# A state-space scan and a routed expert layer: rows turned by transposes, logits in column tiles, one-hots of places on ScalarE, first halves without zero blocks

## The chip, the cores and the metric

The kernel runs on one core of a Trainium2 chip. The metric is the device time of one execution in microseconds; the time of a kernel is the median of several executions. A profile is taken of one further execution, and every time inside the kernel below comes from it, counted from the start of its span.

## The reference

Two layers follow each other. The first is a chunked state-space scan over 4 batches, 8 heads, 768 steps, head width 32, state width 16. Per chunk:

```
cum = cumsum(log a);  L = exp(cum_i - cum_j), lower triangle
y   = ((C B^T) * L) x  +  (C state) * exp(cum)
state = exp(sum log a) * state + sum_j B_j x_j exp(cum_last - cum_j)
```

Its output, seen as 3072 rows (batch, step) of 256 columns (head, width), goes to a router with 8 experts:

```
logits = normalised rows @ normalised expert_emb^T / tau
e      = argmax(logits);  gate = softmax(logits)[e]
out    = gate * (relu(row @ w1[e]) @ w2[e])        # 256 -> 1024 -> 256
```

All is float32.

## The kernel before, in words

**Scan.** The 768 steps are cut in 6 blocks of 128 (`c`), each over all 4 batches and 8 heads. The loop is in `mamba` (L745 to L849), and its order is written out by hand[...]. A block has these steps. `load` brings C, B (two layouts) and x by SyncE's queue; x comes whole as `x`, and the second half of its columns for the first 64 steps once more as `xa`, on partitions 64 to 127 (L68). `scale_c` (VectorE, L254) multiplies C by the decays that `spread_decays` put in PSUM. `inner` (TensorE, L362) makes the products of C and B for two batches at a time in `pg`; `mask_inner` (VectorE, L372) takes them out as `g`, 128x1536. A block has two of these, g(c,0) and g(c,1); the second `inner` of a block waits for `scale_c` of the next. `scale_x` and `scale_first_half` (GpSimd, L276, L289) scale x by inverse decays, into `xs` and `xb`. `from_states`, `outputs` and `first_outputs` (L383, L400, L413) sum y, transposed, in `py`: columns on partitions, in the order (half row r, half v, width), 128 per half z. `first_outputs` is for the first 64 steps of a block: `xb` holds for each head pair a block with zeros in it, so that one product of 128x64 weights gives two heads. Two `xb` buffers are cleared once each, by `clear_first_half` on VectorE. `keep_outputs` (ScalarE, L424) takes y out as `yT`. The states are carried through `sums`, `add_sums` (`V`, VectorE), `decay_states` (`T` on VectorE, `U` on GpSimd, L324).

**Rows and routing.** `finish` (L427) of a block stands in the next block: 8 products of `yT` with `turn` (L432), a matrix that both turns and reorders the columns and holds the normalised expert vectors beside them, so that 128 columns and 8 logits come out together. `keep_rows` (ScalarE, L441, L443) and `send_rows` write rows of 264 columns to memory. `pick` (VectorE) finds each row's expert, `count_picks` (GpSimd) and `rank_rows` (TensorE) its rank; `keep_ranks` (ScalarE, L578) takes that out. `places` (VectorE, L581 to L617) turns the rank into a place: `ge`, `pl`, `eq`, and last `hot`, a one-hot of 104 places for 4 batches (L614). It stands at the end of block c for the rows of block c-2. `locate` (TensorE, L624) multiplies `hot` with `eq` into a table of row numbers, 104 places by 32 (expert, tile), in bank `pz[0]`; ScalarE keeps it (`keep_located`), GpSimd adds (`add_located`). In the last block `early_places` (L913) reads row numbers from the first three blocks' table for the first experts' rows, before g(5,0) in VectorE's queue.

**Scan's end and experts.** `scan_end` (L853) mixes the last blocks' routing with the first expert job: `first.up(f)` (8 products with w1, L1045, relu on ScalarE, L1049), then `down(0)`, `down(1)` (L1063). Their PSUM banks `eb` rotate over 4 buffers: turn_x, up 0 to 7, turn_x of the second job, down(0), down(1), so that down(0) takes the bank that up(5) had. `places` of block 3 stands in the loop's last round, of blocks 4 and 5 in `scan_end`; `locate` of blocks 3 and 4 follows up(3), of block 5 down(0), and `end_places` (L643) makes the final table `idx`. The experts (`moe`, L1315 on) then run one after another, each with rows gathered by GpSimd's indirect transfers, weights through `load_weights` (w1 in two pieces of 64 partitions, L94) and rows scattered to the output.

Of the kernel before, what the change touches and what calls it, by code (L numbers as in the profile page):

```python
# [51 lines left out]
def load(k, c):  # L52
    nc = k.nc
    t = k.ld[c]

    def in_(name, shape):
        return k.inp.tile([128] + shape, F32, name=name, tag=name)

    t.ct, t.bi, t.b = in_("ct", [NB, Q]), in_("bi", [NB, Q]), in_("b", [NB, 128])
    t.x, t.xa = in_("x", [NB, DM]), in_("xa", [NB, 128])  # L60
    def whole(dst, src):
        nc.sync.dma_start(dst[:].rearrange("p b m -> p (b m)"), src[c])

    whole(t.ct, k.CT)
    if c < 2:
        whole(t.bi, k.BT)
    whole(t.x, k.x)
    nc.sync.dma_start(t.xa[HQ:, :, :], k.x[c, 0:HQ, :].rearrange("p (b m) -> p b m", b=NB)[:, :, 128:])  # L68
    whole(t.b, k.B)
    if c >= 2:  # L70
        whole(t.bi, k.BT)
# [8 lines left out]


def load_weights(k, e, parts=(0, 1), after=None):
    nc = k.nc
# [7 lines left out]
    if 0 in parts:  # L91
        k.w1t[e] = k.wp.tile([128, KD, F], F32, name="w1", tag="w1")
        for v in range(2):
            d = nc.sync.dma_start(  # L94
                k.w1t[e][64 * v : 64 * v + 64],
                k.w1[i, 128 * v : 128 * v + 128, :].rearrange("o (z p) f -> p (o z) f", z=KD),
            )
            if after is not None:
                hold(k, d, after)
# [7 lines left out]
def build_consts(k):  # L107
# [41 lines left out]
    keep(k.mask[:, HQ:].rearrange("p (v i) -> p v i", v=2), [[0, 2], [1, HQ]], HQ)  # L149
    k.xb = [mc.tile([128, NB, 4, 2, D], F32, name=f"xb{i}") for i in range(2)]  # L150
    k.half = pool.tile([128, NT], F32, name="half")
    nc.gpsimd.memset(k.half[:], 0.5)


def clear_first_half(k, i):
    k.nc.vector.memset(k.xb[i][0:HQ, :, :, 1, :], 0.0)
    k.nc.vector.memset(k.xb[i][HQ:, :, :, 0, :], 0.0)

# [69 lines left out]
def turn_inverses(k, kk, ps):  # L228
    for i in range(2):
        k.nc.tensor.transpose(  # L230
            ps[:, 128 * i : 128 * i + 128],
            k.rr[kk][:, 2 * i : 2 * i + 2, :].rearrange("p h s -> p (h s)"), k.ident[:],
        )
    k.nc.scalar.copy(out=k.rT[:, kk].rearrange("p i m -> p (i m)"), in_=ps)


def r_of(k, c, i):
    return k.rT[:, c // 4, i, c % 4 : 128 : 4]

# [33 lines left out]
def scale_x(k, c, engine):  # L273
    t = k.ld[c]
    t.xs = k.work.tile([128, NB, DM], F32, name="xs", tag="xs")
    engine.tensor_tensor(  # L276
        out=t.xs[:].rearrange("p b (h d) -> p b h d", h=NH), in0=t.x[:].rearrange("p b (h d) -> p b h d", h=NH),
        in1=r_of(k, c, 1).rearrange("p (b h) -> p b h", b=NB).unsqueeze(3).to_broadcast([128, NB, NH, D]),
        op=ALU.mult,
    )  # L280


def scale_first_half(k, c, engine, halves=(0, 1)):
    t = k.ld[c]
    r = r_of(k, c, 0).rearrange("p (b h) -> p b h", b=NB)
    for v in halves:
        src = (t.x[0:HQ, :, 0:128], t.xa[HQ:, :, :])[v]
        p = slice(HQ * v, HQ * v + HQ)
        engine.tensor_tensor(  # L289
            out=k.xb[c % 2][p, :, :, v, :], in0=src.rearrange("p b (q d) -> p b q d", q=4),  # L290
            in1=r[p, :, 4 * v : 4 * v + 4].unsqueeze(3).to_broadcast([HQ, NB, 4, D]), op=ALU.mult,
        )

# [113 lines left out]
def first_outputs(k, c):  # L407
    t = k.ld[c]
    for b in range(NB):
        for z in range(2):  # L410
            for r in range(2):
                q, o = 2 * z + r, 64 * r
                k.nc.tensor.matmul(  # L413
                    k.py[o : o + 64, z, Q * b : Q * b + HQ],
                    lhsT=k.xb[c % 2][:, b, q].rearrange("p v d -> p (v d)"), rhs=t.g[b // 2][:, q, b % 2, 0:HQ],
                    start=False, stop=True, tile_position=(0, o), skip_group_check=True,
                )

# [6 lines left out]


def finish(k, c, parts=(0, 1)):  # L427
    yT = k.ld[c].yT
    banks = (((2, k.py[:, 0]), (3, k.py[:, 1])), ((0, k.pz[0]), (1, k.pz[1])))
    for b, ps in [x for p in parts for x in banks[p]]:  # L430
        for z, at in ((0, 0), (1, LG)):
            k.nc.tensor.matmul(  # L432
                ps[:, at : at + Y1], lhsT=yT[:, z, b, :], rhs=k.turn[:, z, :],
                start=(z == 0), stop=(z == 1), skip_group_check=True,
            )
# [25 lines left out]
def square_emb(k):  # L461
# [4 lines left out]
    nc.gpsimd.tensor_tensor(out=r[:], in0=r[:], in1=k.half[0:E, 0:1], op=ALU.pow)  # L466
    k.turn = k.mc.tile([128, KD, Y1], F32, name="turn")
    for z, at in ((0, 0), (1, E)):
        nc.gpsimd.tensor_copy(
            out=k.turn[:, z, at : at + 128].rearrange("p (v r d) -> p v r d", v=2, r=2),  # L470
            in_=k.ident[:].rearrange("p (r v d) -> p v r d", r=2, v=2),
        )

# [16 lines left out]
def turn_emb(k, ps):  # L490
# [3 lines left out]
    for z in range(KD):  # L494
        nc.tensor.transpose(ps[:, E * z : E * z + E], k.en2[:, z, :], k.ident[:E, :E])
    for z, at in ((0, 128), (1, 0)):
        nc.scalar.copy(out=k.turn[:, z, at : at + E], in_=ps[:, E * z : E * z + E])


def route_consts(k):  # L500
# [28 lines left out]
    k.s1 = k.const.tile([128, NU], F32, name="s1")  # L529
    k.idx = k.const.tile([TR, E * NT], F32, name="idx")  # L530
    k.shifted = k.mc.tile([128, E], F32, name="shifted")
    nc.gpsimd.memset(k.shifted[:], 0.0)
# [48 lines left out]
def places(k, c):  # L581
# [18 lines left out]
    nc.vector.scalar_tensor_tensor(  # L600
        out=p[:], in0=p[:], scalar=-float(TR), in1=k.s1[:, u], op0=ALU.mult, op1=ALU.add
    )
    nc.vector.tensor_tensor(out=v[:], in0=v[:], in1=p[:].unsqueeze(2).to_broadcast(be), op=ALU.subtract)
    eq = k.eq[c] = w.tile([128, NB * E, NT], F32, name="eq", tag="eq")
# [8 lines left out]
    hot = k.hot[c] = w.tile([128, NB, TR], F32, name="hot", tag="hot")  # L613
    nc.vector.tensor_tensor(  # L614
        out=hot[:], in0=k.place_at[:].unsqueeze(1).to_broadcast([128, NB, TR]),
        in1=p[:].unsqueeze(2).to_broadcast([128, NB, TR]), op=ALU.is_equal,
    )  # L617


def locate(k, c, first=True, last=True):  # L620

    eq, hot = k.eq.pop(c), k.hot.pop(c)
    for b in range(NB):
        k.nc.tensor.matmul(  # L624
            k.pz[0][:TR, 424 : 424 + E * NT], lhsT=hot[:, b, :],
            rhs=eq[:].rearrange("p (b e) t -> p b (e t)", b=NB)[:, b], start=(first and b == 0),
            stop=(last and b == NB - 1), skip_group_check=True,
        )


def keep_located(k, c):
    i = k.idx
    if c > 0:
        i = k.ix = k.work.tile([TR, E * NT], F32, name="ix", tag="ix")
    k.nc.scalar.copy(out=i[:], in_=k.pz[0][:TR, 424 : 424 + E * NT])


def add_located(k, c):
    if c > 0:
        k.nc.gpsimd.tensor_tensor(out=k.idx[:], in0=k.idx[:], in1=k.ix[:], op=ALU.add)  # L640


def end_places(k):  # L643
    nc = k.nc
    n = k.pz[1][:, 456 : 456 + E]
    nc.tensor.matmul(n, lhsT=k.ones[:], rhs=k.pre[:, NU, :], start=True, stop=True)
    nc.vector.tensor_tensor(out=k.idx[:], in0=k.idx[:], in1=k.pz[0][:TR, 424 : 424 + E * NT], op=ALU.add)
    k.gi = k.const.tile([TR, E * NT], I32, name="gi")
# [56 lines left out]
def mamba(k):  # L705
    nc = k.nc
    k.f = k.mc.tile([128, 2, FX], F32, name="f")
    k.rT = k.mc.tile([128, 2, 2, 128], F32, name="rT")
    k.V = k.mc.tile([128, NB, 2 * D], F32, name="V")
# [9 lines left out]
    warm_up(k, 12)  # L719
    clear_first_half(k, 0)  # L720
    decays(k, 0)
# [23 lines left out]
    for c in range(NC):  # L745
# [49 lines left out]
        if c == 0:  # L795
            between(k, n, 4)
            scale_first_half(k, n, nc.gpsimd, (0,))
        elif n < NC:
# [12 lines left out]
        if c == 0:  # L811
            clear_first_half(k, 1)
            spread_decays(k, 2)
# [33 lines left out]
        if c == 0:  # L847
            scale_first_half(k, n, nc.gpsimd, (1,))
            pass_c(k, n)  # L849
# [63 lines left out]
def early_places(k, c):  # L913

    nc = k.nc
    ps = k.pz[0][:TR, 424 : 424 + E * NT]
    locate(k, c)
    nc.vector.tensor_tensor(out=k.idx[:], in0=k.idx[:], in1=ps, op=ALU.add)
    gi = k.ep.tile([TR, E * NT], I32, name="gi0")
    nc.vector.tensor_scalar(out=gi[:], in0=k.idx[:], scalar1=-1.0, scalar2=0.0, op0=ALU.add, op1=ALU.max)  # L920
    k.gi0 = gi
# [564 lines left out]
def leftover(k):  # L1486
# [7 lines left out]
    with k.tc.If(blocks > 0):  # L1494
# [22 lines left out]
        with k.tc.For_i(0, blocks, 1) as i:  # L1517
            e = nc.values_load(table[0:1, 0, bass.ds(i, 1)], engines=(SP,), min_val=0, max_val=E - 1)
            w1 = k.wp.tile([128, KD, F], F32, name="w1", tag="w1")
            for v in range(2):  # L1520
                nc.sync.dma_start(
                    w1[64 * v : 64 * v + 64], k.w1[bass.ds(e, 1), 128 * v : 128 * v + 128, :].rearrange(
                        "o (z p) f -> p (o z) f", z=KD
                    )
                )
            w2 = k.wp.tile([128, KF, DM], F32, name="w2", tag="w2")
# [135 lines left out]
```

## Time and profile before

| | |
|---|---|
| runs | 257.67, 257.88, 259.47 us; median 257.88 |
| profiled execution | 257.48 us, span 255.6 us |
| granted TensorE clock | 0.998 |
| expert products of 208 columns, two records each | 339 to 350 ns a record, one every 176 ns |
| DMA | 35.90 MB, 140 GB/s over the span; 262 GB/s in 11.6 to 31.0 us |
| chain that ended last | TensorE 46%, GpSimd 19%, issue 17%, VectorE 11%, DMA 5% |

The time of the profiled execution is 1.88 us longer than its span. A float32 matrix product shows as two records, a float32 transpose as one, each with its weight load (PEld). Two engines' rows overlap in time; what an engine waited for stands in brackets at the end of a timeline row, as idle time and the one that released it. The scan lasts to about 66 us, the rest is experts, of which the first overlaps the scan's end.

### The profile page before, as it was taken

The page shows a single profiled execution, that of the slowest core. Times are in us where ns is not written, and L with a number is a line of the kernel's source. Part 1 is how long each engine was busy: PE and PEld are TensorE (multiplying, and loading weights), DVE is VectorE, ACT ScalarE, POOL GpSimd, SP SyncE. Part 2 cuts the span into 40 slices and gives each one's busy share as a digit, 9 for nine tenths or more (in the row PEclk, how much of TensorE's full clock was granted, in tenths as well). Part 3 has the DMA queues.
Part 4 walks back from the last instruction along what each step waited for, and adds up shares of the span by engine and source line. Part 5 has one row for each costly group of instructions (what it writes and reads, how often), then busy time and mean ns, then how long its engine had stood idle before and what let it go on. Part 6 is the DMA issues. An engine that isn't in the chain of part 4 may idle for free.

```text
span 255.6 us, 6715 instructions
## 1 busy us (share of the span) xinstructions
PE 240.7 (94%) x2589; PEld 222.5 (87%) x2590; DVE 174.7 (68%) x467; ACT 109.8 (43%) x308; POOL 128.4 (50%) x173
## 2 busy tenths in 40 slices
PE   7889889998999999999999999999999999999990
PEld 2577778878899999999989999999998999999890
DVE  6776898899655533152978897897987888884121
ACT  2435335353254232341385175367338527538300
POOL 8899564764712552838171168248417526026032
PEclk9999999999999999999999999999999999999999
DMA  4978847327299469698911682393194202001001
GB/s 119 306 227 264 279 111 213 131 84 170 65 293 266 151 140 270 147 258 202 255 49 36 135 244 72 88 253 107 39 250 142 69 0 54 11 0 52 13 18 40
DMA packets 22322, 35.90 MB, mean 140 GB/s; under 512 B 2553, under 2 KB 15556, under 8 KB 22288
## 3 DMA queue, kind: packets, MB, share of 16 engines
q1 hardware_dynamic: 19024, 28.73, 41.1%
q0 software_dynamic: 3088, 6.67, 9.8%
q8 instruction: 21, 0.34, 0.6%
q14 instruction: 13, 0.11, 0.1%
q10 hardware_dynamic: 176, 0.06, 0.1%
HBM read 29.05 MB, written 6.50 MB: 139 GB/s over the span
## 4 chain that ended last, share of the span: by engine, by line
PE 46%; POOL 19%; issue 17%; DVE 11%; DMA 5%; ACT 1%; POOLq 1%; DVEq 0%; ACTq 0%
PE yp L1204 15%; PE yp L1132 8%; PE hp L1132 5%; PE eb L1045 5%; DMA out_dram<-yo,to 5%; PE eb L1063 4%; POOL xb L289 4%; POOL xg L934 3%; DVE g L372 3%; POOL out_dram L1255 2%; POOL xs L276 2%; POOL spread L121 1%; PE yp L1032 1%; PE pz L624 1%; PE hp L1045 1%
## 5 line engine op out<-in xcount | busy, mean ns | idle before, releaser
L1255 POOL DMA_INDIRECT out_dram<-yo,to x32 | 34.0, 1063 | 65.1 <-ACT yo L1252 37.2
L934 POOL DMA_INDIRECT xg<-y_rows,gi x32 | 37.3, 1166 | 17.1 <-issue 8.8
L372 DVE TENSOR_TENSOR g<-pg,mask 128x1536 f32<-128x1536 f32 x12 | 21.1, 1754 | 5.5 <-PE pg L362 5.5
L1150 ACT ACTIVATE hT<-hT 128x416 f32<-128x416 f32 (+5 forms) x36 | 19.0, 532 | 12.4 <-DVE hT L1154 11.4
L1063 PE MATMUL yp<-hT,w 128*128 128x208 f32 (+1 forms) x128 | 22.1, 329 | 0.5 <-ACT hT L1150 0.5
L1063 PEld LDWEIGHTS yp<-hT,w 128*128 128x128 f32 x128 | 21.1, 190 | 0.8 <-ACT hT L1150 0.8
L1204 PE MATMUL yp<-T,S 128*128 128x208 f32 (+4 forms) x120 | 21.8, 331 | 0.0
L1282 POOL TENSOR_TENSOR gr<-gr,half 104x4 f32<-104x4 f32 x8 | 9.8, 1219 | 22.0 <-ACT sq L1276 21.9
L1154 DVE TENSOR_TENSOR hT<-hp,u 128x416 f32<-128x416 f32 (+5 forms) x24 | 13.3, 564 | 10.6 <-PE hp L1132 6.5
L1204 PEld LDWEIGHTS yp<-T,S 128*128 128x128 f32 x120 | 20.4, 190 | 0.0
L1132 PE MATMUL yp<-T,S 128*128 128x208 f32 (+5 forms) x96 | 18.6, 336 | 0.4 <-DVE S L1089 0.2
L1132 PEld LDWEIGHTS yp<-T,S 128*128 128x128 f32 x96 | 15.4, 190 | 1.6 <-ACT u L1145 1.1
L1204 PE MATMUL yp<-hT,w 128*128 128x208 f32 (+4 forms) x80 | 15.1, 331 | 0.0
L1145 ACT COPY p<-yp 128x416 f32<-128x416 f32 (+5 forms) x12 | 5.7, 479 | 21.4 <-PE yp L1132 21.4
L1204 PEld LDWEIGHTS yp<-hT,w 128*128 128x128 f32 x80 | 13.7, 190 | 0.0
L1276 ACT ACTIVATE sq<-xg 104x256 f32<-104x256 f32 x32 | 13.0, 408 | 0.0
L1045 PE MATMUL eb<-xT,w 128*128 128x208 f32 x64 | 12.8, 345 | 0.0
L424 ACT COPY yT<-py 128x512 f32<-128x512 f32 x12 | 6.4, 589 | 14.6 <-PE py L413 14.6
L1045 PE MATMUL hp<-xT,w 128*128 128x208 f32 x64 | 12.2, 339 | 0.0
L1063 PE MATMUL eb<-hT,w 128*128 128x208 f32 x64 | 12.0, 341 | 0.0
L1145 ACT COPY u<-yp 128x416 f32<-128x416 f32 (+5 forms) x24 | 11.5, 485 | 1.3 <-PE yp L1132 1.1
L1101 DVE TENSOR_TENSOR T<-hT 128x832 f32<-128x832 f32 (+4 forms) x10 | 9.8, 984 | 3.0 <-ACT hT L1150 3.0
(264 smaller groups left out, 581.3 us busy)
## 6 DMA issues: line engine op xcount, KB each, us to landing
w<-in_moe_w_dram SPq DMA_DIRECT2D x16, 512.0 KB, 6.3
w<-in_moe_w_dram SPq DMA_DIRECT2D x8, 1024.0 KB, 8.2
y_rows<-rows SPq DMA_DIRECT2D x6, 528.0 KB, 5.0
x<-in_x_dram SPq DMA_DIRECT2D x6, 512.0 KB, 6.4
ct<-in_CT_dram SPq DMA_DIRECT2D x6, 256.0 KB, 5.7
bi<-in_BT_dram SPq DMA_DIRECT2D x6, 256.0 KB, 2.8
b<-in_B_dram SPq DMA_DIRECT2D x6, 256.0 KB, 5.2
xa<-in_x_dram SPq DMA_DIRECT2D x6, 128.0 KB, 5.0
```

Of the source, the lines that this page charges most:

```text
L289: engine.tensor_tensor(out=k.xb[c % 2][p, :, :, v, :], in0=src.rearrange("p b (q d) -> p b q d", q=4), in1=r[p, :, 4 * v : 4 * v + 4].unsq ...
L372: t.masked = k.nc.vector.tensor_tensor(out=g[:], in0=k.pg[:, :, 0:384].rearrange("p q (u m) -> p q u m", u=2), in1=k.mask[:].unsqueeze(1). ...
L934: k.nc.gpsimd.indirect_dma_start(out=x, out_offset=None, in_=k.y_d[0:rows, :], in_offset=bass.IndirectOffsetOnAxis(ap=at, axis=0), bounds_ ...
L1045: nc.tensor.matmul(t, lhsT=s.w1[:, j, 128 * f : 128 * f + 128], rhs=s.xT[:, j, 0:m], start=(j == 0), stop=(j == KD - 1))
L1063: nc.tensor.matmul(t, lhsT=s.w2[:, f, 128 * j : 128 * j + 128], rhs=s.hT[:, f, r], start=(f == 0), stop=(f == KF - 1))
L1132: nc.tensor.matmul(t[:, m * u : m * u + m], lhsT=w[:, f : f + 128], rhs=x, start=start and u == 0, stop=True, skip_group_check=True,)
L1145: nc.scalar.copy(out=p[:, 0 : 2 * m], in_=t[:, 0 : 2 * m])
L1150: nc.scalar.activation(h, h, ACT.Relu)
L1154: nc.vector.tensor_tensor(out=h, in0=view(t), in1=view(p), op=ALU.add)
L1204: nc.tensor.matmul(t, lhsT=a[:, f], rhs=b[:, f], start=start and f == 0, stop=(f == 3), skip_group_check=True)
L1255: d = nc.gpsimd.indirect_dma_start(out=k.out[:, :], out_offset=bass.IndirectOffsetOnAxis(ap=s.to[:p, i : i + 1], axis=0), in_=y[:p], in_of ...
L1276: s.k.nc.scalar.activation(sq[:], s.x[:, i, :].rearrange("p (j w) -> p j w", j=KD)[:, :, 0:128], ACT.Square, accum_out=s.r[:, i : i + 1],)
```

## The change

Seven things change together.

- `load`: instead of `xa` there is `xh`, all heads' x for the first 64 steps, on partitions 0 to 63 the first four heads and on 64 to 127 the other four: two transfers instead of one.
- `scale_first_half`: one GpSimd operation of 128x512 makes `xb` without zero blocks; the cleared buffers are gone. Its inverse decays `rh` are copied out of PSUM in two pieces, and `rT` has only the other half (three ScalarE copies instead of one).
- `first_outputs`: 32 products with weights of 64x32 in tiles of the array, instead of 16 of 128x64.
- `finish`: y is turned by 8 transposes, in its own column order; so `w1`'s rows are loaded in that order, in four pieces of 32 partitions. Logits are made transposed, by 8 products of 32 columns in four column tiles, with `emb_t` as weights; ScalarE copies them out (`lt`), and four small products turn them beside the rows.
- `places`: `hot` is made on ScalarE, by four activations (x - place) squared with the place as a per-partition operand, and one relu(1 - 2 x^2) over all. `pl` has the other sign.
- `locate`: `eq` gives the weights, in a column tile for each batch, so that the table comes out as four quarters of partitions, 104 columns. `table` (new) adds them on VectorE and folds the quarters by a product with `same`; it is used in `early_places` and `end_places`. GpSimd builds `same` before the first block's x.
- The order of the steps is otherwise kept.

```diff
@@ def load
-    nc.sync.dma_start(t.xa[HQ:, :, :], k.x[c, 0:HQ, :].rearrange("p (b m) -> p b m", b=NB)[:, :, 128:])
+    for v in range(2):
+        nc.sync.dma_start(
+            t.xh[HQ * v : HQ * v + HQ], k.x[c, 0:HQ, :].rearrange("p (b v m) -> v p b m", b=NB, v=2)[v]
+        )
@@ new function, used by load_weights and leftover
+def w1_rows(k, t, i):
+    issued = []
+    for v in range(2):
+        rows = k.w1[i, 128 * v : 128 * v + 128, :].rearrange("o (z r d) f -> r d (o z) f", z=KD, r=2)
+        for r in range(2):
+            p = 64 * r + 32 * v
+            issued.append(k.nc.sync.dma_start(t[p : p + 32], rows[r]))
+    return issued
@@ def scale_first_half
-    for v in halves:
-        src = (t.x[0:HQ, :, 0:128], t.xa[HQ:, :, :])[v]
-        p = slice(HQ * v, HQ * v + HQ)
-        engine.tensor_tensor(
-            out=k.xb[c % 2][p, :, :, v, :], in0=src.rearrange("p b (q d) -> p b q d", q=4),
-            in1=r[p, :, 4 * v : 4 * v + 4].unsqueeze(3).to_broadcast([HQ, NB, 4, D]), op=ALU.mult,
-        )
+    t.xb = k.work.tile([128, NB, 4, D], F32, name="xb", tag="xb")
+    engine.tensor_tensor(
+        out=t.xb[:].rearrange("p b q d -> p (b q) d"), in0=t.xh[:].rearrange("p b (q d) -> p (b q) d", q=4),
+        in1=k.rh[:, c // 4].rearrange("p b m -> p (b m)")[:, c % 4 : 64 : 4].unsqueeze(2).to_broadcast([128, 4 * NB, D]),
+        op=ALU.mult,
+    )
@@ def first_outputs
-                q, o = 2 * z + r, 64 * r
-                k.nc.tensor.matmul(
-                    k.py[o : o + 64, z, Q * b : Q * b + HQ],
-                    lhsT=k.xb[c % 2][:, b, q].rearrange("p v d -> p (v d)"), rhs=t.g[b // 2][:, q, b % 2, 0:HQ],
-                    start=False, stop=True, tile_position=(0, o), skip_group_check=True,
-                )
+                for v in range(2):
+                    q, p, o = 2 * z + r, HQ * v, 64 * r + 32 * v
+                    k.nc.tensor.matmul(
+                        k.py[o : o + 32, z, Q * b : Q * b + HQ], lhsT=t.xb[p : p + HQ, b, q, :],
+                        rhs=t.g[b // 2][p : p + HQ, q, b % 2, 0:HQ], start=False, stop=True, tile_position=(p, o),
+                        skip_group_check=True,
+                    )
@@ def finish, and new turn_rows
-        for z, at in ((0, 0), (1, LG)):
...
-                ps[:, at : at + Y1], lhsT=yT[:, z, b, :], rhs=k.turn[:, z, :],
+def turn_rows(k, c, b, ps):
+    for z, at in ((0, 0), (1, Y1)):
+        k.nc.tensor.transpose(ps[:, at : at + 128], k.ld[c].yT[:, z, b, :], k.ident[:])
+    if 0 in parts:
+        for b in (2, 3):
+            turn_rows(k, c, b, banks[b])
+        l = k.py[:, 0, W : W + 128]
+        for z in range(KD):
+            for b in range(NB):
+                k.nc.tensor.matmul(
+                    l[32 * b : 32 * b + 32], lhsT=k.emb_t[:, z, :], rhs=t.yT[:, z, b, :], start=(z == 0),
+                    stop=(z == 1), tile_position=(0, 32 * b), skip_group_check=True,
+                )
+        t.lt = k.work.tile([128, 128], F32, name="lt", tag="lt")
+        k.nc.scalar.copy(out=t.lt[:], in_=l)
+    if 1 in parts:
+        for b in (0, 1):
+            turn_rows(k, c, b, banks[b])
+        for b in (2, 3, 0, 1):
+            p = slice(32 * b, 32 * b + 32)
             k.nc.tensor.matmul(
+                banks[b][:, LG : LG + E], lhsT=t.lt[p], rhs=k.ident[p, 32 * b : 32 * b + E], start=True, stop=True,
+                tile_position=(32 * b, 0), skip_group_check=True,
             )
@@ def places
-    nc.vector.tensor_tensor(
-        out=hot[:], in0=k.place_at[:].unsqueeze(1).to_broadcast([128, NB, TR]),
-        in1=p[:].unsqueeze(2).to_broadcast([128, NB, TR]), op=ALU.is_equal,
-    )
+    for b in range(NB):
+        nc.scalar.activation(hot[:, b, :], k.place_at[:], ACT.Square, bias=p[:, b : b + 1])
+    nc.scalar.activation(hot[:], hot[:], ACT.Relu, bias=1.0, scale=-2.0)
@@ def locate
-            k.pz[0][:TR, 424 : 424 + E * NT], lhsT=hot[:, b, :],
-            rhs=eq[:].rearrange("p (b e) t -> p b (e t)", b=NB)[:, b], start=(first and b == 0),
-            stop=(last and b == NB - 1), skip_group_check=True,
+            k.pz[0][32 * b : 32 * b + 32, 400 : 400 + TR],
+            lhsT=eq[:].rearrange("p (b e) t -> p b (e t)", b=NB)[:, b], rhs=hot[:, b, :], start=first, stop=last,
+            tile_position=(0, 32 * b), skip_group_check=True,
@@ new function, used by early_places and end_places
+def table(k):
+    k.nc.vector.tensor_tensor(out=k.idx_t[:], in0=k.idx_t[:], in1=k.pz[0][:, 400 : 400 + TR], op=ALU.add)
+    t = k.pz[1][:TR, 464 : 464 + E * NT]
+    k.nc.tensor.matmul(t, lhsT=k.idx_t[:], rhs=k.same[:], start=True, stop=True, skip_group_check=True)
+    return t
```

## The prediction

> **What bounds the kernel now.** I read the page's first two parts, then the busy time by stage, the chain of waits, and the timeline of one scan block and of the scan's end. Busy time of each engine, and TensorE and ScalarE in 40 slices of 6.4 us:
>
> ```profile
> PE 240.7 (94%) x2589; PEld 222.5 (87%) x2590; DVE 174.7 (68%) x467; ACT 109.8 (43%) x308; POOL 128.4 (50%) x173
> ...
> PE   7889889998999999999999999999999999999990
> ...
> ACT  2435335353254232341385175367338527538300
> ```
>
> From 66 us on TensorE never rests: the stage view counts 15.40 busy us in 66.4 to 81.8, 166.63 of 173.8 in the rest. So the time is when the expert products begin, plus a fixed train: a us won or lost before 85 us is one at the end. ScalarE's 43% says nothing on 66 to 82 us.
>
> Block c=3 of the scan, in the timeline (start, us, engine, line, out<-in):
>
> ```profile
> 36.58 1.08 POOL L289 TENSOR_TENSOR xb<-xa,rT 64x512 f32<-64x512 f32 x1
> 36.81 0.87 DVE L594 TENSOR_TENSOR ge<-s,first_of 128x12 f32<-128x12 f32 x1
> 37.73 0.62 POOL L267 TENSOR_TENSOR cp<-cp,ends 128x256 f32<-128x256 f32 x1
> 37.91 0.45 DVE L600 SCALAR_TENSOR_TENSOR pl<-pl,s 128x4 f32<-128x4 f32 x1
> 39.17 0.58 DVE L614 TENSOR_TENSOR hot<-place_at,pl 128x416 f32<-128x416 f32 x1
> 40.16 0.62 POOL L324 TENSOR_TENSOR U<-T,ends 128x256 f32<-128x256 f32 x1 [1.81 <-DVE T L318]
> 41.22 1.75 DVE L372 TENSOR_TENSOR g<-pg,mask 128x1536 f32<-128x1536 f32 x1
> ```
>
> The reader is to see one VectorE queue, g, places, T, (U on GpSimd), V, next g, that sets the 10.3 us of a block, and two operations of 12 and 4 columns that end with GpSimd's (37.68 with 37.66, 38.36 with 38.35). At 69.12 the same ge takes 0.17. GpSimd then waits 1.81 us for VectorE.
>
> The scan's end, ScalarE between TensorE's products:
>
> ```profile
> 73.47 0.34 ACT L1049 ACTIVATE hT<-eb 128x208 f32<-128x208 f32 x1 [0.32 <-PE eb L1045]
> ...
> 76.36 0.34 ACT L1049 ACTIVATE hT<-eb 128x208 f32<-128x208 f32 x1 [1.45 <-PE eb L1045]
> ...
> 77.28 0.34 ACT L1049 ACTIVATE hT<-eb 128x208 f32<-128x208 f32 x1 [0.49 <-PE eb L1045]
> ...
> 78.84 3.00 PE L1063 MATMUL eb<-hT,w 128*128 128x208 f32 x16
> ```
>
> From 69.24 to 79.03 ScalarE waits only some 3 us in all (its brackets: 0.28, 0.58, 0.32, 1.45, 0.49). That is all the room it has.
>
> **What the skill says.** "SBUF — State Buffer", Who interferes with whom: a VectorE operation with two SBUF inputs and a GpSimd one that reads SBUF exclude each other for a whole instruction. The trace agrees (above). "ScalarE: Activation LUTs", What ACT_TABLE_LOAD costs: an activation with constants is 186 ns + 0.833 per column, each per-partition operand adds about 93, and neighbours overlap by about 93. The trace agrees: 128x416 takes 0.556, the scaled 128x64 copy 0.344. "TensorE: Matmul & The Clock Gate", LDWEIGHTS: a load's time goes with its columns. The trace agrees: 32-column loads (L400) follow each other at 15.5 ns, 64-column ones (L413) at 31.6, 104-column ones (L624) at 87. The SBUF page's Door 1 lets 32 partitions reach as many ports as 64; no row of before shows it.
>
> **The change, part by part.**
>
> 1. Loads. 128 KB more per block, one more issue on SP (0.6 us, ahead of b). The second ct lands last at 11.96 (VectorE waits 0.22 for it). 128 KB at the 262 to 306 GB/s of that stage: +0.45, on the path. It covers the start: two memsets fewer (0.97 us) and turn copies for the quarters' sum on GpSimd (-0.4, +1.1: xs(0) 0.7 later, and outputs(0,0) still ends before g(0,1) frees pg).
>
> 2. xb. One 128x512 operation for two of 64x512. Time goes with columns (128x256 0.62, 128x1024 1.97): 1.07, bounds 0.62 and 1.97. Saves 1.1 us of GpSimd a block.
>
> 3. First halves on TensorE: 64 records of 64x32 tiles for 32 of 128x64. At 15.5 ns: 0.99 for 1.01. Bounds: 7.8 ns (two row halves at once) 0.5; 31.6 ns, 2.0. I take no change.
>
> 4. finish. Before, 16 records at 0.116: 1.86. After: 8 transposes at 0.11 (two of L1249 in 0.22): 0.88; logits, 16 records of 128 columns, 107 ns each by the 0.83 ns a column of L1045, four columns of tiles at once: 0.43; 8 small records at 27 ns: 0.22. Sum 1.53, but with a trip through ScalarE: lt, about 0.28 between rk's 0.19 and hT's 0.34, in order behind whatever is queued there.
>
> 5. Table products: 8 records at 87 ns before, 0.70; after 8 x 87 / 4: 0.2. New: idx_t added on VectorE and a product by the folded identity, twice, about 0.7 of latency with TensorE waiting.
>
> 6. One-hots leave VectorE (0.58) for ScalarE: four squares with a pointer, 0.186+0.093+0.087 = 0.37 each (estimate by the page named), 0.28 apart; the relu of 416 columns 0.55, which waits for the last square: 1.12+0.16+0.47 = 1.75 us a block. Bounds: 1.25 (no pointer cost, at relus' 0.24 spacing), 2.1 (no overlap). What queues behind: lt, rows, relus; TensorE waits for each.
>
> 7. w1 in four pieces: two more issues of about 0.65 us on SP. The tightest, w1 of the second expert, is issued at 69.65 and used at 85.44, and takes 6.3 to land. Nothing; without this cover, us for us.
>
> **The sum, along the path** (negative: earlier than before).
>
> Start: +0.45. Block 1: finish(0) shorter and T(1) unblocked (0.60 to 0.42), -0.55: -0.10. Block 1 to 2: the second xb no longer sits on decays(1), where a copy of 4 columns takes 1.06 beside it (0.37 alone) and the scan 0.78 (0.62): -0.85: -0.95. Block 2: ge, pl and hot give back some 1.5 on VectorE, but then inner(3,0) on TensorE is last: its chain g, outputs, first halves, sums, inner ends at 40.48 where g began 41.22: -0.7: -1.65. Block 3, likewise, with the kept-out cp still blocking once: -0.85: -2.5. Block 4: hot(2) starts after yT(4) at 58.84+1.0, lasts 1.75, and locate(2), which began at 60.34 before, waits for it, then idx_t and the folded product stand before gi and g(5,0): +1.15: -1.35 at g(5,0).
>
> Scan's end, on before's clock without that shift. ScalarE: yT from 69.24, hot(3) 70.20 to 71.95, relu, rk, relu to 72.55, lt to 72.85. The small products end 73.1, before 72.73. Rows to 74.27, hot(4) to 76.0. Table product 4 ends 76.35, before 75.54. Fourth relu and rk by 77.8; VectorE needs 1.05 from rk to pl (76.82 to 77.83 before); hot(5) 78.9 to 80.65; relu of f=5 to 81.0. down(0) takes that relu's bank: it starts 81.0 where it started 79.01. +2.0. Table product 5 with the folding: 0.85 for 0.67: +0.2. Sum -1.35+2.2 = +0.85.
>
> Against the profiled execution, 257.48 (span 255.6 and 1.88 around it): 258.3. The median of the runs is 0.4 above that execution: 258.7.
>
> **Rivals.**
>
> A. ScalarE keeps up: hot near 1.25 and always under another wait. For: 3 us of room, and TensorE's own work there shrinks, 0.33 in finish and 3 x 0.5 in table products, less 0.5 for the folding: -1.3, on a start at -1.9. -3.2: 254.7. Against: 3 x 1.75 + 0.3 is 5.5 us into 3 us of room.
>
> B. Slower by TensorE: the 64-row tiles do not follow at 15.5 ns. At 31.6 each block's first halves grow 1.0; yT, finish and the next inner stand behind them. Blocks 0, 2, 4, 5 in full, about half hidden in 3, less 0.9 of slack: +3.5 on top, 262.2. It decides from about 24 ns on. Against: 32-column loads of 128 rows keep 15.5.
>
> C. w1 pieces arrive late in the experts: from a landing above 15.8 us; about 261.
>
> D. hot is offloaded but the chain of block 2 to 4 gains nothing since TensorE is last: that is inside the main case's range.
>
> **The numbers.** Main case 0.63, A 0.19, B 0.13, C 0.05. A tenth of a us of hot is worth 0.35 (it counts once in block 4, some 2.5 times in the end), so 1.4 to 2.1 gives 257.5 to 260.0, the main case's own range. The forecast is 258.7. The range, 254.9 to 261.4, cuts off half of A and most of B and C. About 1% (2.6 us) is what a measurement tells from no change. Faster by more: A's greater part and the fastest corner of the main, 0.17; slower: B, C and hot beyond 2.2, 0.22; within, 0.61.
>
> **What would show it.** Right: g(4,0) near 49.1 for 51.55; ge at 0.2 to 0.45; g(5,0) near 60.4; then hot groups on ScalarE of 1.7 to 1.8 us, ahead of relus that no longer wait for eb, idle TensorE between up(3) and the table products and before down(0), down(0) about 0.7 later than 79.01. Wrong: hot near 1.2 and TensorE busy throughout (A); records of the first halves above 24 ns (B); waits of the experts for w (C); g(4,0) not earlier: the VectorE reading fails.

## The result, and the profile after

The changed kernel takes 274.53 us (median of 4, 272.38 to 276.44) where the kernel before takes 258.37 on the same chip: 1.0619 times as long, 95% interval 1.053 to 1.0709. The forecast was 258.7, in a range of 254.9 to 261.4: no change that could be measured. The profiled execution took 276.44. The kernels have a slower state in some executions, at a lower granted clock: medians and ranges here are of all executions and ratios of the faster ones alone, so a ratio need not be the quotient of the medians beside it.

First the page, busy time by engine and the 40 slices (6.9 us each now):

```profile
span 274.7 us, 7381 instructions
...
PE 250.8 (91%) x2882; PEld 225.8 (82%) x2882; DVE 166.6 (61%) x458; ACT 120.1 (44%) x347; POOL 121.7 (44%) x170
...
PE   7895978979878889999999999999999999999991
...
ACT  2421424663435752251325537636635725726500
...
PEclk9977597995799999999999999999999999999999
```

The granted clock of the kernel before, from its page:

```profile
PEclk9999999999999999999999999999999999999999
```

Three things differ. TensorE has 293 matmuls and 292 weight loads more. It has holes, of which the largest are in slices 4, 6, 9 and 12. And the granted clock, 9 in every slice before, drops to 5 and 7: that line was never a topic of the prediction.

Second, where the 19.1 us between the two profiled spans arise. Each row is the distance between two events, from the timelines (g(c,j) is the start of mask product j of block c, up and down TensorE's first product of that name):

```
stretch                         before   after    difference
start to g(1,0)                  17.22   18.70      +1.48
g(1,0) to g(1,1)                  6.30   11.83      +5.53
g(1,1) to g(2,1)                 11.14   13.72      +2.58
g(2,1) to g(4,0)                 16.89   18.20      +1.31
g(4,0) to g(5,0)                 10.14   15.27      +5.13
g(5,0) to the first up            7.38    8.05      +0.67
first up to the second's up      16.21   18.72      +2.51
from there to the end           170.3   170.2       -0.1
```

The scan's end (+2.51 for a forecast +2.2) and the experts behave as forecast. At g(5,0) the kernel is 16.0 us late, where it was to be 1.35 early.

Third, the worst place, block 1 in the timeline of the changed kernel (start, us, engine, line, then in brackets the idle time before and who ended it):

```profile
22.98 0.30 PE L448 MATMUL py<-yT,emb_t 128*32 128x128 f32 x1
...
24.54 1.07 POOL L294 TENSOR_TENSOR xb<-xh,rh 128x512 f32<-128x512 f32 x1
...
25.88 1.08 PE L448 MATMUL py<-yT,emb_t 128*32 128x128 f32 x15 [2.60 <-issue]
...
30.53 1.76 DVE L378 TENSOR_TENSOR g<-pg,mask 128x1536 f32<-128x1536 f32 x1 [7.93 <-PE pg L368]
```

TensorE stops for 2.60 us between the first and the second of sixteen alike matmuls, which wait for nothing new. "issue" means that the profile has no releaser. VectorE then waits 7.93 us for TensorE. The waits of TensorE, summed:

```profile
PE pz L652 <- ACT hot L645: 2.6, 2, 1.6
PE py L448 <- issue: 2.6, 1, 2.6
PE pg L196 <- issue: 1.6, 1, 1.6
...
PE pg L368 <- issue: 1.4, 1, 1.4
```

Besides the forecast wait for the one-hots (hot) there are 5.6 us of waits for nobody in these three lines, which have no more in common than being TensorE's. The kernel before had one of that kind:

```profile
PE py L383 <- issue: 0.3, 1, 0.3
```

Fourth, the part of the DMA view on instructions, and what its packets say. Queue q8 has one packet of 16 KB for each 256 of TensorE's instructions, so I take it for the one that brings them:

```profile
q8 instruction: 23, 0.38, 0.6%
```

I counted TensorE's records in the trace (loads, matmuls, semaphore instructions) up to each stop, and put the packets of q8 beside them. A batch is 256 instructions, a boundary the count at which one begins. "Asked" is when TensorE went past the boundary before, 256 instructions earlier:

```
changed kernel  boundary   asked   packet           TensorE stops and resumes
                   449     13.97   16.66 to 17.98   18.87 to 19.54
                   705     19.54   23.34 to 24.40   23.28 to 25.88
                  1217     33.17   35.59 to 36.55   36.44 to 38.03
                  2497     57.62   59.14 to 60.23   60.35 to 61.72
```

All four stops lie at 193 modulo 256, and each ends 1.48 to 1.56 us after its packet: I read this as TensorE having run out of instructions, which the experiments test. They are 6.2 us together. At the other boundaries of the scan the packet had ended at least 2.1 us earlier, and there is no stop.

Fifth, the clock, in the busy times of stretches (TensorE's busy us first; the last three numbers are clock, DMA share and GB/s):

```profile
10.70:14.10 3.40, 2.36 (x32) 1.73 (x35) 2.12 (x2) 1.32 (x6) 3.09 (x9) 1.00 1.09 310
14.10:17.50 3.40, 3.40 (x96) 2.93 (x92) 1.76 (x1) 1.43 (x4) 2.88 (x3) 0.50 1.08 254
20.90:24.30 3.40, 1.77 (x61) 1.19 (x50) 1.51 (x4) 1.07 (x2) 2.84 (x3) 1.00 1.08 316
24.30:27.70 3.40, 1.82 (x19) 1.31 (x18) 0.00 (x0) 0.27 (x1) 1.88 (x3) 0.51 0.66 151
27.70:31.10 3.40, 3.40 (x58) 2.95 (x60) 0.57 (x1) 2.52 (x7) 0.00 (x0) 0.50 0.01 2
31.10:34.60 3.50, 3.50 (x107) 3.00 (x103) 3.26 (x13) 0.23 (x1) 0.00 (x0) 0.50 0.75 263
34.60:38.00 3.40, 1.84 (x92) 1.47 (x85) 1.26 (x4) 1.46 (x4) 2.54 (x2) 1.00 1.10 303
```

The reader is to see that a stretch with holes (2.36 and 1.77 busy of 3.40) is followed by half clock, in steps of 3.41 us. Up to the last microseconds the clock was halved four times, from 14.12, 24.36, 44.84 and 61.90 on, for 3.41, 10.24, 3.41 and 10.24 us, 27.3 together. Only the two long ones begin behind a stop of the table above. Before the short ones TensorE waited for others: 0.72 us up to 13.53 for `scale_c`, and 0.97 up to 42.46 for ScalarE's rows. The rule isn't one of busy time alone: 34.6 to 38.0 has a hole too and keeps its clock afterwards. The same 32 products with the states at half and at full clock:

```profile
30.38 1.98 PE L389 MATMUL py<-cp,T 32*64 32x128 f32 x32
80.63 1.10 PE L389 MATMUL py<-cp,T 32*64 32x128 f32 x32
```

### The profile page after: what moved, and what is told of

Same layout as the page of the kernel before. It is cut to its first block, busy times and chain, and to the rows that moved or that the text cites. A ratio compares the mean times of both kernels' runs of the same rounds, so it can differ in the third digit from the quotient of the medians.

```text
span 274.7 us, 7381 instructions
## 1 busy us (share of the span) xinstructions
PE 250.8 (91%) x2882; PEld 225.8 (82%) x2882; DVE 166.6 (61%) x458; ACT 120.1 (44%) x347; POOL 121.7 (44%) x170
## 4 chain that ended last, share of the span: by engine, by line
PE 49%; issue 18%; DVE 8%; DMA 8%; POOL 8%; ACT 6%; SPq 1%; POOLq 1%; DVEq 0%; ACTq 0%
PE yp L1236 14%; PE yp L1164 7%; PE hp L1164 4%; PE eb L1095 4%; DMA out_dram<-yo,to 4%; POOL xg L966 4%; PE pg L368 3%; PE eb L1077 2%; DMA ct<-in_CT_dram 2%; PE py L406 2%; PE py L420 2%; POOL out_dram L1287 2%; ACT hot L644 2%; DMA xg<-y_rows,gi 2%; DVE g L378 1%
## 5 line engine op out<-in xcount | busy, mean ns | idle before, releaser
L368 PE MATMUL pg<-cp,bi 32*128 32x128 f32 x192 | 12.8, 337 | 1.4 <-issue 1.4
L1236 PEld LDWEIGHTS yp<-hT,w 128*128 128x128 f32 x80 | 13.7, 190 | 0.0
L584 POOL TENSOR_TENSOR pre<-pre,ob 128x8 bf16<-128x8 bf16 x24 | 4.8, 200 | 18.3 <-DVE ob L579 16.8
L284 POOL TENSOR_TENSOR xs<-x,rT 128x1024 f32<-128x1024 f32 x6 | 11.8, 1966 | 2.5 <-ACT rT L242 1.9
```

Of the source, the lines that this page charges most:

```text
L284: engine.tensor_tensor(out=t.xs[:].rearrange("p b (h d) -> p b h d", h=NH), in0=t.x[:].rearrange("p b (h d) -> p b h d", h=NH), in1=r_of(k ...
L368: k.nc.tensor.matmul(k.pg[:, q, 192 * u + a : 192 * u + a + n], lhsT=m, rhs=x, start=True, stop=True, tile_position=(32 * q, 0),)
L1236: nc.tensor.matmul(t, lhsT=a[:, f], rhs=b[:, f], start=start and f == 0, stop=(f == 3), skip_group_check=True)
```

## The experiments

Theory F: TensorE's instructions come in batches of 256 (16 KB), each asked for as the one before is begun; the packet is held up by the loads in the DMA engines; the change's more numerous instructions use a batch up sooner than the next one lands. After such a hole comes half clock. Rivals: L, the extra loads are late; S, ScalarE's new work; K, narrow tiles by themselves lower the clock.

**Instruction count alone** (before_split). The kernel before; each first-half product of 128x64 weights cut into two of 128x32:

```
-  lhsT=k.xb[c % 2][:, b, q].rearrange("p v d -> p (v d)")          # 128x64, into py[o : o + 64]
+  for v in range(2): lhsT=k.xb[c % 2][:, b, q, v, :]               # 128x32, into py[o + 32 * v : ...]
```

> The kernel before with one edit: each first-half product of 128x64 weights becomes two of 128x32, so TensorE gets 192 more loads and 192 more matmuls (32 of each in each of six blocks) for the same column time; loads, GpSimd, ScalarE and VectorE stay. Theory F (TensorE runs out of instructions: a batch of 256 is not there in time): stalls of 0.5 us or more without any releaser, at instruction counts that differ by multiples of 256, half clock after them; 262 to 275 us. Theory L (the extra rows of x make loads late): 258, no change. Theory K (the narrow tiles themselves count as low activity and lower the clock): slower by 3 us or more, half clock without such stalls.

266.98 us where the kernel before took 257.68, ratio 1.0308 (1.0218 to 1.0398). From its timeline:

```profile
30.36 0.44 PE L362 MATMUL pg<-cp,bi 32*128 32x128 f32 x4
35.24 0.58 PE L362 MATMUL pg<-cp,bi 32*128 32x128 f32 x2 [4.44 <-issue]
```

Stops at counts 449, 705, 1217 and 1729, 10.3 us in all; the packet for 1217 was asked for at 28.21 and began at 32.90. From g(1,0) to g(2,0) this kernel takes 19.95 us and before 13.80: 6.15 more, as much as the two stops there, 1.71 and 4.44. L and S have no hand in it, as neither a load nor an operation of ScalarE differs. K falls too: the clock is halved from 33.02 on, within the stop of 4.44 us, and from 50.09 on, behind that of 3.06; from 53.50 it is full to 265, with the narrow products of blocks 4 and 5 in between.

**The same without the loads** (before_split_noload), `if c >= 2:` the tiles of block c-2 stand in for the loads.

> The kernel before with each first-half product in two of 128x32, and without the loads of blocks 2 to 5 (they take the inputs of blocks 0 and 1, so their values are others; nothing else is left out). TensorE's instructions are as many as in the run with the loads. If the batches of instructions are late because they stand behind the loads in the DMA engines: the stalls after 25 us go (there were 4.4 and 3.1 us), a batch starts within 1.3 us, and the twelfth mask product starts near 65 us in place of 76. If TensorE's fetch is slow by itself: the stalls stay at the same instruction counts.

Only the scan is read: with other values what stands behind it is another job (466.01 us for the whole, one execution). The boundary at 1217 again:

```profile
27.72 0.44 PE L366 MATMUL pg<-cp,bi 32*128 32x128 f32 x4
28.50 0.38 PE L366 MATMUL pg<-cp,bi 32*128 32x128 f32 x2 [0.34 <-issue]
```

4.44 us became 0.34, 3.06 at 1729 became 0.87, and the twelfth mask product starts at 67.13 instead of 76.09. So the batches are late because of the loads; whether they queue in the DMA engines or behind the memory, the run doesn't tell. And not all of it is the loads: with quiet DMA too the batch for 1729 was there only 2.87 us after it was asked for (37.47 to 40.34), and TensorE had used up the one before in 2.0.

**The changed kernel with parts undone.** after_joined puts the zero blocks and 128x64 tiles back; after_noxh takes xb from `t.x[:, :, 0:128]`; after_hot_dve has one comparison on VectorE for the four squares and the relu.

> The changed kernel with its first halves joined again (128x64 weights with zero blocks, two GpSimd operations of 64 partitions, the two clearing memsets back), everything else of the change kept, the extra load too. Theory F: 192 loads and 192 matmuls fewer, so most of the stalls without a releaser go, and half clock with them; 256 to 263. Theory L: the late loads stay, 270 to 275. A theory S (one-hots on ScalarE and the logits' trip cost the time): 272 to 276.

> The changed kernel without the loads of xh; xb is made from the columns that x has in the same partitions, so the first halves of half the heads are wrong in value, and nothing else is left out. TensorE's instructions stay as many. Theory F: the 256-instruction batches still come late, somewhat less so with 256 KB a block fewer in the queues; 264 to 273, stalls without a releaser still there. Theory L: the loss was the loads', so it goes; 256 to 260.

> The changed kernel with the places' one-hots back on VectorE (one comparison of 416 columns and one small sign change in place of four squares and a relu on ScalarE). Theory F: the blocks keep their stalls, only the scan's end gets back its wait for the one-hots, some 2 us; 270 to 274. Theory S: most of the loss goes, under 264.

Medians 267.19 (263.96 to 270.38), 271.41 (267.09 to 273.25) and 268.45 (ratio 1.0415, 1.0334 to 1.0495), each against 257.68. Joined: even the fastest execution is beyond the range that F gave; stops stay at 1729 and 2241 (0.8 and 1.0 us), and half clock for 3.41 and 6.83 us, from 35.48 and 66.20 on, so not behind these stops. Without xh: even the fastest is 7 us above L's range, and the stops at 705, 1217 and 2497 are there again (1.8, 2.3, 1.0), so L falls; with half the heads' values wrong the experts' part may differ. One-hots back: some 5 us (1.0415 for 1.0619) and not 2, more than F allowed for. From g(4,0) to g(5,0) it takes 10.28 for 15.27. But the wait for the one-hots isn't all that went there: the stop at 2497 is 0.6 us for 1.4, and the half clock that began behind it at 61.90, ahead of that wait, is gone. So these 5 us don't belong to S alone. S is a share of its own and not the main one: more than 10 of the 16 us stay without it.

**Two parts undone** (after_joined_dve, both edits above).

> The changed kernel with two parts undone: first halves joined again and the one-hots back on VectorE; left are the logits in column tiles with their trip through ScalarE, the products by quarters and the extra rows of x. Theory F for the scan blocks with theory S for the rest (one-hots on ScalarE cost what the prediction said, 2 to 3.5 us, plus half clock after their wait): 257 to 260. If the parts that are left cost something themselves: 261 to 265.

265.65 for 259.94, ratio 1.0159 (1.0075 to 1.0243): what is left costs some 4 us, with stops at four boundaries (0.5 to 1.2 us). Hence each part alone.

**The parts alone, on the kernel before.** before_hot_act moves the one-hots, before_xh the loads, before_finish the rows and logits (with w1's order), before_quarters the table products.

> The kernel before with one edit: the places' one-hots on ScalarE, four squares and a relu per block. The prediction's step 6 alone: groups of 1.75 us, the wait in the fifth block and the two at the scan's end, +1.5 to +3.5, so 259.5 to 261.5, all of it after 60 us; no stalls without a releaser, as TensorE's instructions are as many as before. A rival (ScalarE's order alone throws the scan off as the whole change did): 265 or more.

> The kernel before with the change's loads alone: both halves of the first rows of x come by transfers of their own (128 KB a block more, one more issue), and its two GpSimd operations read them. TensorE's instructions stay. Prediction: +0.45. Theory F, at the edge: batches of 256 instructions land 0.02 to 0.3 us ahead of use in four places of before, so later ones give short stalls without a releaser; +0.5 to +3. If only the narrow tiles matter: 0 to +0.5.

> The kernel before with the change's rows and logits alone (transposes, logits in column tiles with their copy by ScalarE, and w1 in the row order that it needs, in four pieces). By the prediction's price of TensorE's time: -0.3 a block, so -1 to +0.5. By theory F: 32 instructions a block more (16 records for 32 of loads and matmuls each), some stalls without a releaser; +1 to +4.

> The kernel before with the table products alone by quarters of the array, folded by one product of their own. By the prediction: three waits of 0.5 us less, two of 0.7 more; -0.5 to +0.5. Theory F has nothing against it, as TensorE's instructions are as many.

```
part alone           median   before   ratio (interval)            us        forecast of the part
first halves' count  266.98   257.68   1.0308 (1.0218 to 1.0398)   +7.9      0
one-hots             262.63   259.94   1.0098 (1.0070 to 1.0127)   +2.5      +1.5 to +3.5
rows and logits      261.71   259.87   1.0087 (1.0060 to 1.0113)   +2.3      -0.3 a block
table products       260.54   259.87   1.0036 (1.0001 to 1.0070)   +0.9      about 0
loads                260.68   259.87   1.0008 (0.9981 to 1.0035)   +0.2      +0.45
```

(us is ratio less one, times the median before. By the medians it is 9.3, 2.7, 1.8, 0.7 and 0.8.) The sum is 13.8 of the 16.0 that the whole costs; as each part shifts the boundaries of the others, such a sum is no proof that they add. Rows and logits have 16 matmuls and 16 loads a block more, and stops at 961, 1217, 1729 and 2241, 0.6 to 1.1 us each: F again. The loads alone bring stops too, of 1.1 us at 449 and under 0.3 at three more, but no cost that can be told, less than the +0.5 to +3 of F. The table products have one of 0.7 at 2497. The one-hots have TensorE's count of before and no stop at a boundary, but the wait that was forecast:

```profile
59.39 1.20 ACT L615 ACTIVATE hot<-place_at,pl 128x104 f32<-128x104 f32 x4
60.62 0.55 ACT L616 ACTIVATE hot<-hot 128x416 f32<-128x416 f32 x1
...
61.22 0.92 PE L623 MATMUL pz<-eq,hot 128*104 128x32 f32 x8 [1.62 <-ACT hot L616]
```

**Half clock by itself** (after_joined_fill): seven matmuls of ones, `warm_up(k, 7)`, fill the wait for the one-hots ahead of g(5,0). The kernel that it is added to is after_joined.

> The changed kernel with joined first halves, and seven matmuls of ones (512 columns, bf16, results never read) put ahead of the table product in the last block, where TensorE waits 1.62 us for the one-hots. Nothing is left out. If half clock follows TensorE's idleness: none from that point on where the kernel without them had 6.8 us of it, and the last block 1 to 3 us shorter. If half clock comes from the small tiles or from the page stalls alone: no change, or up to 1.5 us longer.

The stretch from 66 to 73 us, without and with them:

```profile
66.00:73.00 7.00, 7.00 (x143) 5.90 (x135) 4.66 (x12) 1.43 (x4) 5.41 (x9) 0.51 0.18 50
```

```profile
66.00:73.00 7.00, 5.77 (x141) 4.12 (x138) 4.69 (x10) 1.70 (x5) 3.70 (x7) 1.00 0.28 69
```

The filled hole kept the clock, as expected; the gain did not come. The kernel takes 268.49 us (264.38 to 274.39) where before took 259.94 on that chip, and from g(4,0) to the first up it is 21.01 us for 20.98. In that stretch TensorE is not last. These are GpSimd's gathers of the first expert's rows in the filled run, the first of which waits for the indices and the last of which the first up stands behind:

```profile
68.15 1.31 POOL L975 DMA_INDIRECT xg<-y_rows,gi  x1 [4.21 <-DVE gi L961]
69.77 1.08 POOL L975 DMA_INDIRECT xg<-y_rows,gi  x1 [0.30 <-issue]
...
72.50 1.09 POOL L975 DMA_INDIRECT xg<-y_rows,gi  x1 [0.57 <-issue]
73.89 1.11 POOL L975 DMA_INDIRECT xg<-y_rows,gi  x1 [0.30 <-issue]
```

With them the chain from the indices on is as long at either clock.

In block 3 half clock does cost, as a run from further below shows. In before_pad36, which leaves nothing out and whose profile has no stop of over 0.13 us at a boundary, three executions of twelve have a granted clock of 0.982 to 0.984 and take 259.6 to 259.7 us; the other nine have 0.989 to 0.998 and take 257.2 to 258.2. The profile is of one of the three:

```profile
30.00:33.40 3.40, 1.96 (x14) 1.51 (x12) 2.76 (x5) 2.08 (x7) 2.54 (x2) 1.00 0.55 163
33.40:36.80 3.40, 3.35 (x56) 3.13 (x60) 2.04 (x6) 1.22 (x4) 2.02 (x6) 0.50 0.04 13
36.80:40.20 3.40, 3.40 (x94) 2.86 (x90) 2.64 (x10) 0.18 (x1) 1.48 (x2) 0.50 0.94 328
```

So 6.83 us of half clock go with some 2 us more. At that rate the 27.3 us of the changed kernel would be 8 to 9 of its 16; that is an estimate, and no run takes the half clock out of the changed kernel's blocks 1 to 3.

**Where the boundaries fall.** The opening matmuls on ones, twelve of 512 columns, are issued as more and narrower ones with the same columns: this shifts every boundary of 256 against the scan and alters nothing else in the program.

```
-    warm_up(k, 12)
+    for _ in range(48):   # before_split_shift, +72 instructions; 84 of 73 columns: +144; 72 of 85: +120; 30 of 205: +36
+        k.nc.tensor.matmul(k.pz[1][:, 0:128], lhsT=k.warm[:, 0:Q], rhs=k.warm[:, 0:128], start=True, stop=True)
```

> The kernel before with first-half products of 128x32, as above, and the twelve opening matmuls of 512 columns issued as forty-eight of 128: 72 instructions more ahead of the scan, for the same columns. Theory F: every stall without a releaser again ends a batch, at counts that differ by multiples of 256 from 449, but at other lines of the scan, so other stalls and another sum; 259 to 272. If the stalls belong to the lines where they stood (a wait that the profile does not show): same lines, counts 72 higher.

> The kernel before with its twelve opening matmuls of 512 columns issued as eighty-four of 73 (64 weights wide): the same columns, 144 instructions more ahead of the scan, nothing else. Theory F: from the times at which before issued each instruction, and a batch taking 2.55 us plus 1.0 (DMA quiet) or 2.3 (busy) from the crossing of the boundary before, boundaries shifted by 144 cost an estimated 4.4 us of stalls where those of before cost 0.8: 260 to 265 where before has 258 to 260. If placement is not decisive: within 1 us of before.

> The kernel before with the opening matmuls as thirty of 205 columns, 36 instructions more. By the same estimate of theory F boundaries shifted by 36 cost 0.1 us for 0.8: 0 to 1 us faster than before, or no change that can be measured.

> The changed kernel with the opening matmuls as seventy-two of 85 columns (64 weights wide), 120 instructions more ahead of the scan, nothing else changed. Theory F: by the same estimate the stalls fall from 6.3 us to 4.0, and some half clock with them; 266 to 272, stalls at the same counts mod 256 but other lines. If the loss is elsewhere in the change: 272 to 277.

> The changed kernel with the one-hots on VectorE and 144 instructions more ahead of the scan (eighty-four opening matmuls of 73 columns). Theory F: the estimate falls from 9.5 us of stalls to 4.9; 260 to 266 where the same kernel without the padding was 4.2% above before. If placement is not decisive: 267 to 270.

before_split_shift: 261.28 for 259.87, ratio 1.0019 (0.9990 to 1.0049), where the same products unshifted had 1.0308. Its stops are at 705 and 1217 again, both now inside the sums, and at 2497 (0.5 us):

```profile
PE pz L333 <- issue: 4.5, 2, 2.3
```

The count stayed and the line moved, so the stops don't belong to lines. But placement is a lesser lever than I had estimated. before_pad144: 258.17 for 257.63, ratio 1.0019 (1.0005 to 1.0033), where 260 to 265 was expected: the stops came (2.1 us at L362), and cost 0.5. That VectorE's chain covers short stops in these blocks would explain it, and isn't shown. before_pad36: 257.69, ratio 1.0010 (0.9985 to 1.0035), nothing. after_pad120: 271.76, ratio 1.0511 (1.0475 to 1.0547), perhaps 3 us of the 16 back (the intervals overlap). That is within F's range, but by luck: the stops were to fall from 6.3 us to 4.0, and its trace has 7.8, 3.3 of them at 1217. What fell is the half clock, from 27.3 us to 13.7. after_hot_dve_pad144: 267.19, ratio 1.0375 (1.0287 to 1.0462), against 1.0415 no gain that can be told, where 260 to 266 was expected. Why one shift saved 3% and another none is open: a batch's delay varies with what the loads are just doing, and I have no model of that. No version tried is faster than the kernel before.

## Why the prediction was wrong

**The step that failed** is part 3, "At 15.5 ns: 0.99 for 1.01. ... I take no change", and with it part 4's "Sum 1.53" for 1.86: both price TensorE's work by the time of its records and give the number of instructions no price. The durations themselves were nearly right: in block 0 the 64 loads (L420) took 0.94 us, 14.7 ns each, and the rows and logits of block 0, by themselves on the kernel before, went from 2.29 us to 1.99: both are more than the 1.86 and 1.53 of the prediction, but the difference is the 0.3 that was forecast. But the first halves' higher count alone costs 7.9 us, and rows and logits with theirs cost 2.3. Rival B had the engine and the sign, and the wrong mechanism: it needed 24 ns a record.

Nothing in the kernel before stood out, yet its trace had the sign of it. Of its batches, those for 449, 705, 961, 2497 and 2753 were begun 1.71, 1.80, 1.27, 1.45 and 1.50 us after their packets' end, and in no profile here did TensorE begin one earlier than 1.15. At these boundaries it had next to no reserve, with 5179 loads and matmuls; the change has 5764.

**The second thing without a price** was the clock. The Trainium skill, "TensorE: Matmul & The Clock Gate" (Part 1: The HAM clock gate), says that idleness of TensorE halves its clock, judged in windows of 3413 ns; the trace agrees, with its stretches of 3.41 and 10.24 us at 0.50. It differs in how little idleness that takes, as the stretches ahead of half clock are 52 to 71% busy, and in the way back: from 27.7 to 34.6 us TensorE was busy throughout and stayed at half clock. So a hole may be paid for again later.

**The other steps.** Start: the second ct ends VectorE's wait at 12.79 for 11.96, +0.83 for +0.45; alone the loads cost 0.2 us (-0.5 to +0.9). GpSimd: xb takes 1.07 to 1.08, as forecast, and VectorE's small operations are free of it as forecast: ge takes 0.17 to 0.19 in all six blocks, where it took up to 0.87. That was to bring g(4,0) to 49.1; it came at 62.45, because TensorE, not VectorE, was last: the 2.5 us that were to be gained up to there lay in a chain that no longer set the time. For the kernel before the reading has some support: with the one-hots alone moved off VectorE (before_hot_act), g(4,0) comes at 50.80 for 51.55. One-hots: 74.54 to 76.32 is 1.78 us for 1.75; the wait in block 4 came, 1.64 us:

```profile
74.54 1.20 ACT L644 ACTIVATE hot<-place_at,pl 128x104 f32<-128x104 f32 x4
75.77 0.55 ACT L645 ACTIVATE hot<-hot 128x416 f32<-128x416 f32 x1
...
76.37 0.39 PE L652 MATMUL pz<-hot,eq 128*32 128x104 f32 x8 [1.64 <-ACT hot L645]
77.21 0.37 PE L675 MATMUL pz<-same,idx_t 128*104 128x32 f32 x2 [0.46 <-DVE idx_t L673]
```

The table product is 0.39 for a forecast 0.2, and the folding behind it costs 0.83 (0.46 of waiting, 0.37 of its own) for about 0.7. Scan's end: first up to first down takes 11.84 for 9.77, +2.07 where +2.0 was forecast, with the relu in front of it as said:

```profile
97.61 3.08 PE L1095 MATMUL eb<-hT,w 128*128 128x208 f32 x16 [0.92 <-ACT hT L1081]
```

w1 in four pieces: nothing, the train after it is 170.2 us for 170.3.

So most terms that I worked out from durations held to some tenths of a us. The answer was wrong by 16 mainly because a resource that has no row among the engines was left out, the supply of instructions, and with it the clock; how the 16 us divide between stops and half clock stays open.

## What to carry to other kernels

When a change multiplies TensorE's instructions, count them: 256 of them in less time than a batch takes to come (here an estimated 4 us as a rule, 2.5 to the packet's end and 1.5 more, and up to 7.7, the longer while loads fill the DMA engines) stop the engine, however short each one is. A wait of TensorE that the profile puts down to "issue" in the middle of equal matmuls is the sign. It isn't proof by itself, as before_hot_act has such waits of up to 0.5 us away from any boundary: compare the counts modulo 256 and the packets of the instruction queue. And read the clock's line after each change: a hole can halve it for 3 to 10 us, which costs where TensorE is last and nothing where, as here before the first expert, gathers are.

## What the runs showed of the hardware

Of each of the 18 profiles I took the first twelve batches that a packet brought, 216 in all. Where the DMA engines were quiet in the microsecond after the boundary before was crossed (share under 0.3, 72 batches), the packet began a median of 0.9 us after the crossing; where they were full (over 0.8, 108 batches), 2.0 us, up to 4.7. In 14 of the 216 it began before the crossing, by up to 1.2 us. The packet itself took 0.9 to 2.2 us, 1.1 as a rule, and no batch was begun earlier than 1.15 us after its packet. At 49 of these boundaries TensorE stopped for over 0.35 us, and 48 of the stops ended 1.15 to 1.63 us after the packet (in three runs, where a record seems to be missing, at 192 modulo 256). So in these kernels the supply is asked for about one batch ahead. The Trainium skill, "Runtime: NRT & Kernel Launch" (Instruction fetch mechanics), gives blocks of 16 KiB, 256 instructions, fetched by a DMA queue of the engine's own, and the trace agrees (0.38 MB in 23 packets). It calls the cost mostly hidden, and here the measurement decides: up to 4.44 us in one place.
